# Chunk groups across batches, an accumulator as fifth bank in the last block, and residuals formed by identity products

## The chip, the core and the metric

The kernel runs on one core of a Trainium2 chip. The metric is device microseconds (us) of one execution; the median of three runs is given, and one further execution was profiled. The engines are PE (matmuls; PEld is its weight loads), DVE, ACT, POOL (elementwise work) and SP, which issues nearly all DMAs. Each engine works through its own list of instructions in order.

## The reference, cut to what matters

```
attn: out[b,s,h,:] = sum_k softmax(weight)[h,k] * x[b, s-6+k, h,:]     # B,S,D = 2,4096,192; 8 heads, 7 taps
layer 1: h = x @ w_in;  g = max(0.01*h, h);  x = g @ w_out              # 8192 tokens, 192 -> 2048 -> 192
layer 2: h = x @ w_in2
         P = a0 + a1*h + a2*h^2 + a3*h^3
         Q = 1 + |b0|*|h| + |b1|*h^2
         out = (P / (Q + 1e-6)) @ w_out2
```

All is float32; the weights arrive as 64-bit floats and are converted by the kernel.

## The kernel before, in words

The 8192 tokens are 16 blocks of 512. Hidden units are 16 tiles of 128 (index j). For each block i, layer and tile, `gemm1` (5 matmuls of 128x512) forms the hidden tile h in one of four PSUM banks (pool `bank`), the elementwise engines turn h into a high part gH and a remainder gL (pool `pair`), and `gemm2_hi` (3 matmuls, of gH) and `gemm2_lo` (2, of gL) add them into two accumulators: `acc[0]` in layer 1 (`acc[1]` for block 1), `acc[1]` in layer 2. So a tile costs PE ten matmuls. `middle(i)` (`mid_swap`, `x_hi` on ACT, `mid_add`, `x_lo` on DVE) splits layer 1's result into the operands of layer 2, and `finish(i)` (`fin_*`) transposes and stores layer 2's.

Elementwise work of a layer 2 tile: ACT forms two affine or absolute values of h (`l2_vp`), DVE the denominator's core D (`l2_D`), ACT `l2_abs`, then `l2_rs` and `l2_R` (R = 1/(D+QC)), DVE `l2_p2`, `l2_p3` (numerator without a0, written over h in the bank) and `l2_hi` (gH). The remainder is gL = (h + a0 - (D+QC)*gH) * R: `l2_Q` adds QC to D (ACT or POOL), `l2_w` multiplies by gH (POOL), `l2_r` subtracts (DVE), `l2_lo` multiplies by R (POOL). In the last block (i = 15) the tiles in `GPDEN` form D with `l2_up`, `l2_t` (ACT) and `l2_ut` (POOL) in place of `l2_D` and `l2_abs`; tiles in `ENDW` and `ENDV` may have `l2_w` and `l2_lo` on DVE.

The convolution is a product with a band matrix. Blocks 0 and 1 (`DIRECT`) make it in place; for the rest, chunks of 122 tokens are taken in groups of up to five (`group`): load, `conv_g` (two halves; on PE each is four float32 matmuls, which the trace shows as eight), `evac_g`, and a store to DRAM, from where each block fetches its columns.

The weights come as 28 pieces (14 for each layer): a load, two DVE steps `cv_clip` and `cv_bits` of two instructions each, and splits into high and low parts. Before the first data arrive, `s_warm` runs matmuls on constants.

Order: every step is put into a planner with the engines that it may run on and a rank, made of due times (`LEAD`, `GAP`, `STEP`, `CV1` to `CV3`) and a table of offsets (`OFF`). The planner writes each engine's list once, while the program is built. Layer 2 of a block runs beside layer 1 of the blocks behind it, so the last block's layer 2 has no layer 1 beside it.

## Time and profile before

| | |
|---|---|
| median of 3 runs (lowest, highest) | 1244.76 us (1244.41, 1244.92) |
| profiled execution, whole | 1244.22 us |
| its span in the trace | 1242.4 us |
| mean granted clock of PE, as a share of full speed | 0.996 |
| busy share: PE, DVE, ACT, POOL | 98%, 90%, 92%, 85% |

The span reaches from the first to the last recorded instruction; 1.8 us of the execution lie around it. A matmul's recorded time overlaps the next one's, so 98% for PE does not say that it never waits.

### The profile page before, as it was taken

How to read it: one execution, taken by the hardware profiler on the slowest of the kernel's cores; microseconds unless marked ns; L12 is line 12 of the kernel's file. 1: busy time of each engine (PE TensorE's matmuls, PEld its weight loads, DVE VectorE, ACT ScalarE, POOL GpSimd, SP SyncE). 2: the span in 40 equal slices, each digit the busy share in tenths (PEclk: the TensorE clock that was granted, in tenths of full speed). 3: DMA queues.
4: the chain of work that ended last, by engine and by line, in shares of the span. 5: the costliest groups of instructions: out<-in, count | busy, mean ns of one | idle time of the engine just before them, and what ended most of it. 6: DMA issues, size and time to landing. Idle time of an engine off the chain costs nothing.

```text
span 1242.4 us, 17891 instructions
## 1 busy us (share of the span) xinstructions
PE 1217.3 (98%) x5437; PEld 997.6 (80%) x5437; DVE 1112.0 (90%) x1671; ACT 1138.5 (92%) x1996; POOL 1059.2 (85%) x1000
## 2 busy tenths in 40 slices
PE   8999999999999999999999999999999999999976
PEld 7787788888888888888888888888888888888744
DVE  7999989898998989898988999898998989889898
ACT  6889999899999999999999999999999999999996
POOL 2787988989889898898888989899898888988886
PEclk9999999999999999999999999999999999999998
DMA  7752002020110201111010111010210002000000
GB/s 210 200 164 71 1 3 52 2 42 1 38 18 1 56 1 44 18 30 33 7 45 12 29 33 29 20 23 5 50 26 1 13 1 41 1 1 14 1 13 13
DMA packets 137414, 42.34 MB, mean 34 GB/s; under 512 B 113571, under 2 KB 134758, under 8 KB 137318
## 3 DMA queue, kind: packets, MB, share of 16 engines
q1 hardware_dynamic: 135702, 41.00, 14.3%
q8 instruction: 42, 0.69, 0.2%
q14 instruction: 54, 0.44, 0.1%
q10 hardware_dynamic: 1616, 0.21, 0.1%
HBM read 27.28 MB, written 11.80 MB: 31 GB/s over the span
## 4 chain that ended last, share of the span: by engine, by line
PE 81%; ACT 7%; DVE 7%; issue 2%; DMA 1%; POOL 1%; SPq 0%; POOLq 0%; DVEq 0%; ACTq 0%
PE bank L253 41%; PE acc L253 39%; ACT work L244 4%; DVE work L250 2%; ACT raw L244 1%; DMA raw<-in_moe_w_in_dram 1%; DVE bank L250 1%; DVE pair L247 1%; ACT bank L244 1%; DVE bank L396 1%; DVE bank L397 1%; DVE pair L250 1%; DVE work L247 0%; DVE raw L250 0%; POOL pair L247 0%
## 5 line engine op out<-in xcount | busy, mean ns | idle before, releaser
L253 PE MATMUL acc<-pair,wo 128*128 128x512 f32 x2560 | 657.4, 391 | 6.2 <-POOL pair L247 2.7
L253 PEld LDWEIGHTS acc<-pair,wo 128*128 128x128 f32 x2560 | 478.5, 188 | 110.6 <-POOL pair L247 6.9
L244 ACT ACTIVATE work<-work 128x512 f32<-128x512 f32 x532 | 331.4, 630 | 17.6 <-DVE work L250 11.0
L247 POOL TENSOR_TENSOR work<-work,pair 128x512 f32<-128x512 f32 x184 | 239.5, 1302 | 43.6 <-DVE pair L250 34.6
L253 PE MATMUL bank<-xh,wiH 128*128 128x512 f32 x512 | 203.5, 397 | 9.2 <-DVE raw L250 4.2
L253 PE MATMUL bank<-xh,wiL 128*128 128x512 f32 x512 | 200.2, 391 | 0.0
L253 PE MATMUL bank<-xl,wiH 128*128 128x512 f32 x512 | 200.0, 391 | 0.0
L253 PE MATMUL bank<-xl,wiR 128*128 128x512 f32 x512 | 200.0, 391 | 0.0
L253 PE MATMUL bank<-xh,wiR 128*128 128x512 f32 x512 | 199.9, 390 | 0.0
L250 DVE SCALAR_TENSOR_TENSOR work<-work,b_sb,bank 128x512 f32<-128x512 f32 x182 | 135.1, 742 | 46.5 <-ACT work L244 45.3
L247 POOL TENSOR_TENSOR pair<-work,work 128x512 fp32r<-128x512 f32 x122 | 158.0, 1297 | 20.4 <-DVE work L250 14.8
L250 DVE SCALAR_TENSOR_TENSOR work<-bank,a_sb,work 128x512 f32<-128x512 f32 x184 | 136.9, 744 | 9.6 <-POOL work L247 7.6
L244 ACT ACTIVATE work<-bank,a_sb 128x512 f32<-128x512 f32 x176 | 135.3, 769 | 6.1 <-PE bank L253 6.0
L250 DVE SCALAR_TENSOR_TENSOR pair<-bank,a_sb,work 128x512 fp32r<-128x512 f32 x168 | 125.2, 745 | 13.1 <-ACT work L244 7.8
L250 DVE SCALAR_TENSOR_TENSOR bank<-work,a_sb,bank 128x512 f32<-128x512 f32 x176 | 132.1, 752 | 4.1
L244 ACT ACTIVATE raw<-raw 128x512 f32<-128x512 f32 x202 | 126.8, 630 | 6.2 <-DVE raw L250 3.6
L253 PEld LDWEIGHTS bank<-xh,wiH 128*128 128x128 f32 x512 | 96.4, 188 | 38.1 <-DVE raw L250 6.6
L247 POOL TENSOR_TENSOR pair<-work,pair 128x512 fp32r<-128x512 f32 x92 | 120.3, 1308 | 7.0 <-PE acc L253 1.8
L244 ACT ACTIVATE work<-bank,b_sb 128x512 f32<-128x512 f32 x182 | 124.0, 681 | 0.0
L247 DVE TENSOR_TENSOR work<-work,bank 128x512 f32<-128x512 f32 x176 | 119.3, 678 | 1.3 <-ACT raw L244 1.3
L253 PEld LDWEIGHTS bank<-xl,wiH 128*128 128x128 f32 x512 | 96.5, 189 | 20.7 <-DVE xl L247 0.3
L253 PEld LDWEIGHTS bank<-xl,wiR 128*128 128x128 f32 x512 | 96.4, 188 | 20.6 <-DVE xl L247 0.3
(104 smaller groups left out, 1954.5 us busy)
## 6 DMA issues: line engine op xcount, KB each, us to landing
work<-y_dram SPq DMA_DIRECT2D x108, 64.0 KB
raw<-in_moe_w_out_dram SPq DMA_DIRECT2D x16, 384.0 KB
xt<-in_x_dram SPq DMA_DIRECT2D x59, 96.0 KB
y_dram<-xc SPq DMA_DIRECT2D x58, 84.0 KB
raw<-in_moe_w_in_dram SPq DMA_DIRECT2D x8, 512.0 KB
out_dram<-work SPq DMA_DIRECT2D x63, 64.0 KB
raw<-in_moe_w_in_dram SPq DMA_DIRECT2D x8, 256.0 KB
work<-work SPq DMA_DIRECT2D x16, 128.0 KB
```

The lines of the kernel that those rows point to most:

```text
L244: nc.scalar.activation(out=out_, in_=in_, func=func, **k)
L247: (eng or nc.vector).tensor_tensor(out=out_, in0=in0, in1=in1, op=op)
L250: nc.vector.scalar_tensor_tensor(out=out_, in0=in0, scalar=s, in1=in1, op0=op0, op1=op1)
L253: nc.tensor.matmul(out=out_, lhsT=w, rhs=r, start=start, stop=stop)
L396: nc.vector.tensor_scalar(out=a, in0=a, scalar1=F64_TINY, scalar2=F64_HUGE, op0=ALU.max, op1=ALU.min)
L397: nc.vector.tensor_scalar(out=ai, in0=ai, scalar1=3, scalar2=0x3FFFFFF8, op0=ALU.logical_shift_left, op1=ALU.bitwise_and)
```

## The change

- Chunks are listed over both batches first and then cut into groups of five, so a group may hold the end of batch 0 and the start of batch 1. There are 12 groups; before there were 13, five of them with four chunks.
- The warm-up is 13 float32 matmuls on constants in place of 8 and 19 others; the copy that fed the others (`s_seed`, DVE) goes.
- `s_abs` (ACT, waits for the load of b) stands behind more of ACT's first work.
- When layer 1's last block is through, `acc[0][0]` joins the pool `bank` as a fifth bank.
- In the last block, for the tiles in `QPE`, two matmuls with negated identities subtract QC*gH from h in the bank, and `l2_Q` falls away. For those in `WPE`, one float32 matmul with a negated identity subtracts D*gH there, and `l2_end` (DVE) forms gL in place of `l2_r` and `l2_lo`.
- `GPDEN` has eight tiles for four, `ENDW` and `ENDV` eight for one and two; the numbers that make the ranks are others throughout.

```diff
-LEAD = 66.057
-GAP = 6.373
-PREP = 56.276
+LEAD = 75.81
+GAP = 3.101
+PREP = 36.864
...
-CV1, CV2, CV3 = -20.785, 58.237, 26.634
+CV1, CV2, CV3 = -15.913, 176.158, 29.877
...
-GPDEN = (2, 5, 8, 11)
-ENDW = (15,)
+GPDEN = (0, 1, 2, 3, 5, 9, 12, 14)
+ENDW = (1, 2, 4, 5, 7, 9, 12, 14)
...
-ENDV = (14, 15)
+ENDV = (0, 1, 5, 6, 7, 8, 11, 15)
+QPE = (5, 6, 9, 10, 11)
+WPE = (0, 1, 3, 6, 7, 9, 10, 11, 13)
...
+    pl.pool("own", acc[0][0:1])
...
+    groups = [chunks[c:c + NTC] for c in range(0, len(chunks), NTC)]
...
     def s_warm(eng):
         for n in range(WARM):
             mm(acc[0][1][:, 0:WIDE], ident, qc[:, 0:WIDE], True, True)
-        t = xh[1][0][0]
-        for cols, count, step in SHAPES:
-            for n in range(count):
-                k = n * step % 4
-                mm(acc[0][1][:, 0:cols], t[:, k * P:(k + 1) * P], t[:, 0:cols], True, True)
...
+    def l2_sub(eng, i, j, part):
+        h = b("h", 1, i, j)
+        if part:
+            nc.tensor.matmul(out=h, lhsT=neg, rhs=b("D", 1, i, j), start=False, stop=True, skip_group_check=True)
+        else:
+            for t in negQ:
+                nc.tensor.matmul(out=h, lhsT=t, rhs=b("gH", 1, i, j), start=False, stop=True, skip_group_check=True)
+
+    def l2_end(eng, i, j):
+        stt(b("gL", 1, i, j), b("h", 1, i, j), a_sb[:, 0:1], b("R", 1, i, j), ALU.add, ALU.mult)
...
-            on(DVE(t_dve(n, 1)), s, 9.6, l2_r, i, j, r=[h, dk], w=[dk])
-            on(POOL(t_pool(n)) + end, s, 10.6, l2_lo, i, j, r=[dk, rk], w=[gl], take=("pair", gl))
+            if subw:
+                on(PE(2 * (0.0025 + n / 1200.0)), s, 9.6, l2_sub, i, j, 1, r=[dk, "neg"], w=[h])
+                on(DVE(t_dve(n, 1)), s, 10.6, l2_end, i, j, r=[h, rk], w=[gl], take=("pair", gl))
+            else:
+                on(DVE(t_dve(n, 1)), s, 9.6, l2_r, i, j, r=[h, dk], w=[dk])
+                on(POOL(t_pool(n)) + end, s, 10.6, l2_lo, i, j, r=[dk, rk], w=[gl], take=("pair", gl))
```

Three places of the order show what moves.

The first is SP's list of loads behind the third piece of layer 1's `w_in`; `moe2` names layer 2's weights, `moe` layer 1's, `y_dram` and `xt` belong to the convolution. Before:

```order
L373 DMA raw2_128<-in_moe_w_in_dram 128x1024
L377 DMA raw0_126<-in_moe2_w_in_dram 64x1024 x2
L511 DMA work4_107<-y_dram 32x16x32 x4
L511 DMA work7_110<-y_dram 32x16x32 x4
L373 DMA raw1_127<-in_moe2_w_in_dram 128x1024
L379 DMA raw2_128<-in_moe_w_out_dram 128x2x384
L379 DMA raw0_126<-in_moe_w_out_dram 128x2x384
```

And of the change, behind the same load of `w_in` and ten stores of the first group:

```order
L389 DMA raw0_129<-in_moe_w_out_dram 128x2x384
L484 DMA xt0_79<-in_x_dram 128x192 x5
L521 DMA work7_113<-y_dram 32x16x32 x4
L521 DMA work9_115<-y_dram 32x16x32 x4
L389 DMA raw1_130<-in_moe_w_out_dram 128x2x384
L387 DMA raw2_131<-in_moe2_w_in_dram 64x1024 x2
L383 DMA raw0_129<-in_moe2_w_in_dram 128x1024
```

The pieces of layer 2 have moved behind two of layer 1's output weights, and DVE converts the pieces in the order of their loads.

The second is DVE around the last `x_lo` (the rows `xl101` and `xl111`), where block 15 enters layer 2; the row with `acc01` is `mid_add`, a row `pair<-bank` is an `l2_hi`, a row `work<-bank` or `raw<-bank` an `l2_r`, and rows with `b_sb` are `l2_D`. Before:

```order
L250 SCALAR_TENSOR_TENSOR pair0_116<-bank2_101,a_sb_65,raw0_126 128x512
L247 TENSOR_TENSOR work11_114<-work11_114,acc01_96 128x512
L247 TENSOR_TENSOR work3_106<-work3_106,bank0_99 128x512
L247 TENSOR_TENSOR xl101_92<-acc00_95,xh101_84 128x512
L247 TENSOR_TENSOR xl111_94<-work11_114,xh111_86 128x512
L250 SCALAR_TENSOR_TENSOR work7_110<-bank2_101,a_sb_65,work7_110 128x512
L250 SCALAR_TENSOR_TENSOR bank0_99<-work3_106,a_sb_65,bank0_99 128x512
L250 SCALAR_TENSOR_TENSOR pair1_117<-bank0_99,a_sb_65,raw1_127 128x512
L250 SCALAR_TENSOR_TENSOR work2_105<-work2_105,b_sb_66,bank3_102 128x512
```

Of the change:

```order
L251 TENSOR_TENSOR work2_108<-work2_108,acc01_99 128x512
L254 SCALAR_TENSOR_TENSOR pair8_127<-bank2_104,a_sb_68,raw2_131 128x512
L254 SCALAR_TENSOR_TENSOR raw0_129<-bank3_105,a_sb_68,raw0_129 128x512
L251 TENSOR_TENSOR xl101_95<-acc00_98,xh101_87 128x512
L251 TENSOR_TENSOR xl111_97<-work2_108,xh111_89 128x512
L254 SCALAR_TENSOR_TENSOR raw1_130<-bank2_104,a_sb_68,raw1_130 128x512
L251 TENSOR_TENSOR work12_118<-work12_118,bank0_102 128x512
```

Two steps of block 14 stand ahead of the last `x_lo` in place of one, and one of its steps stands behind it in place of four.

The third is PE in the middle of the last block; rows with `wi` are a `gemm1`, rows `acc<-pair` are `gemm2`, rows with `neg` or `negQ` are the new subtractions. Before, the ten matmuls of `gemm2` for two tiles, with the `gemm1` of another between:

```order
L253 MATMUL acc11_98<-pair5_121,wo1_75 128x512
L253 MATMUL acc10_97<-pair5_121,wo1_75 128x512
L253 MATMUL acc10_97<-pair8_124,wo1_75 128x512 x2
L253 MATMUL acc11_98<-pair8_124,wo1_75 128x512
L253 MATMUL bank2_101<-xh101_84,wiH1_69 128x512
L253 MATMUL bank2_101<-xh101_84,wiL1_71 128x512
L253 MATMUL bank2_101<-xl101_92,wiH1_69 128x512
L253 MATMUL bank2_101<-xh111_86,wiR1_73 128x512
L253 MATMUL bank2_101<-xl111_94,wiR1_73 128x512
```

Of the change, ahead of the `gemm1` of tile 12 (it is the row behind the last one here):

```order
L364 MATMUL bank3_105<-work9_115,neg_65 128x512
L257 MATMUL acc10_100<-pair3_122,wo1_78 128x512 x2
L257 MATMUL acc11_101<-pair3_122,wo1_78 128x512
L367 MATMUL bank2_104<-pair2_121,negQ0_66 128x512
L367 MATMUL bank2_104<-pair2_121,negQ1_67 128x512
L257 MATMUL acc11_101<-pair8_127,wo1_78 128x512
L257 MATMUL acc10_100<-pair8_127,wo1_78 128x512
L257 MATMUL acc10_100<-pair9_128,wo1_78 128x512 x2
L257 MATMUL acc11_101<-pair9_128,wo1_78 128x512
L364 MATMUL bank2_104<-work8_114,neg_65 128x512
L367 MATMUL bank0_102<-pair1_120,negQ0_66 128x512
L367 MATMUL bank0_102<-pair1_120,negQ1_67 128x512
```

PE's list holds the subtractions of tiles 7, 9 and 10 between the hidden products of tiles 11 and 12.

## Rows read from the trace of the kernel before

**Rows 1.** The page's busy times: engine, us, share of the span, instructions.
```profile
PE 1217.3 (98%) x5437; PEld 997.6 (80%) x5437; DVE 1112.0 (90%) x1671; ACT 1138.5 (92%) x1996; POOL 1059.2 (85%) x1000
```

**Rows 2.** Busy us (x instructions) by stretch: PE, PEld, DVE, ACT, POOL; PE's clock, DMA.
```profile
40.00:160.00 120.00, 117.53 (x514) 93.78 (x513) 111.70 (x179) 110.20 (x204) 98.80 (x105) 1.00 0.35 97
200.00:1100.00 900.00, 899.83 (x4048) 745.86 (x4047) 807.82 (x1196) 840.04 (x1463) 796.37 (x739) 1.00 0.11 21
1175.03:1236.90 61.87, 49.11 (x176) 32.87 (x174) 57.43 (x87) 55.07 (x94) 52.35 (x45) 0.94 0.04 7
...
1191.10:1194.30 3.20, 2.98 (x7) 2.37 (x8) 3.20 (x6) 2.27 (x5) 3.07 (x3) 0.50 0.00 0
...
1176.10:1206.50 30.40, 24.15 (x86) 16.17 (x86) 28.68 (x46) 28.63 (x49) 25.86 (x23) 0.94 0.08 14
```

**Rows 3.** The chain that ended last: start us, us, what.
```profile
53.65 0.66 DVE pair L247
...
105.23 1.28 ACT L244
...
142.25 1.45 PE bank L253 x5
...
236.77 2.27 PE bank L253 x10
```

**Rows 4.** PE's waits from 36 to 160 us: us in total, times, longest.
```profile
PE bank L253 <- ACT xc L244: 1.2, 2, 0.9
```

**Rows 5.** PE's timeline at two chunk groups: start, us, operation, count.
```profile
104.07 1.01 PE L253 MATMUL bank<-xt,band 128*122 128x120 f32 x8
104.84 0.94 PE L253 MATMUL acc<-pair,wo 128*128 128x512 f32 x3
...
182.73 1.85 PE L253 MATMUL bank<-xt,band 128*122 128x96 f32 x16
184.36 0.93 PE L253 MATMUL acc<-pair,wo 128*128 128x512 f32 x3
```

**Rows 6.** The timeline of the first 15 us, PE and one step of ACT.
```profile
2.50 5.70 PE L253 MATMUL acc<-qc,ident 128*128 128x256 f32 x16 [2.50 <-POOL ident masks.py:199]
7.84 3.01 PE L253 MATMUL acc<-xh 128*128 128x192 f32 x19
12.22 2.09 PE L253 MATMUL bank<-xt,band 109*103 109x120 f32 x16 [1.36 <-DMA b_sb<-in_moe_b_dram]
13.63 0.20 ACT L244 ACTIVATE b_sb<-b_sb 128x2 f32<-128x2 f32 x1 [2.74 <-DMA b_sb<-in_moe_b_dram]
14.15 0.60 PE L253 MATMUL acc<-qc,ident 128*128 128x256 f32 x2
14.59 0.98 PE L253 MATMUL bank<-xt,band 109*103 109x120 f32 x8
```

**Rows 7.** PE's timeline in the last block; in brackets the idle time before.
```profile
1184.95 0.96 PE L253 MATMUL acc<-pair,wo 128*128 128x512 f32 x3 [2.18 <-DVE work L699]
1191.32 0.79 PE L253 MATMUL bank<-xh,wiH 128*128 128x512 f32 x1 [1.60 <-DVE raw L250]
1211.64 0.80 PE L253 MATMUL bank<-xh,wiH 128*128 128x512 f32 x1 [1.74 <-DVE raw L250]
1224.92 0.39 PE L253 MATMUL bank<-xl,wiR 128*128 128x512 f32 x1
```

**Rows 8.** DVE's timeline: last `x_lo`, tile 6's `l2_r`, tile 15's `l2_lo`.
```profile
1175.43 0.68 DVE L247 TENSOR_TENSOR xl<-work,xh 128x512 fp32r<-128x512 f32 x1
1205.76 0.75 DVE L250 SCALAR_TENSOR_TENSOR work<-bank,a_sb,work 128x512 f32<-128x512 f32 x1
1235.29 0.79 DVE L247 TENSOR_TENSOR pair<-raw,work 128x512 fp32r<-128x512 f32 x1
```

**Rows 9.** The last `fin_swap`, and SP's last stores.
```profile
1236.68 0.59 ACT L244 ACTIVATE work<-acc 64x512 f32<-64x512 f32 x1 [4.00 <-PE acc L253]
1237.66 1.65 SPq L720 DMA_DIRECT2D out_dram<-work  x3
```

84 lines of the change are left out of this document (45 added, 39 removed).

## The prediction

> **What bounds the kernel now.** I read the page's busy times first: PE 98%, ACT 92%, DVE 90%, POOL 85% [rows 1]. PE leads, but the share is an average, so the next view is busy time by stretch. From 200 to 1100 us PE is busy for 899.8 of 900 us and starts 4048 matmuls, one in 0.222 us [rows 2]. There only fewer matmuls can save anything. From 40 to 160 us it starts 514; at 0.222 us the 120 us would hold 540, so 26 matmuls, 5.7 us, are lost [rows 2]. In the last block, 1175.0 to 1236.9 us, PE starts 176 [rows 2]: 168 at 0.227 us (ten in 2.27 us [rows 3]) are 38.1 us, 8 of the constant kind at 0.22 us (two in 0.44 us: starts at 14.15 and 14.59 [rows 6]) 1.8 us, so 39.9 us of work and 22.0 us without. DVE is busy for 57.4 of these 61.9 us, ACT for 55.1.
>
> The third view is the chain that ended last. From about 54 to 142 us its pieces are mostly DVE's, from 142 us PE's [rows 3]: the first stage is held by DVE, which converts weights beside layer 1's remainders. So there are three places for a gain: the start, PE's list in the middle, and the last block.
>
> **The change part by part.** Durations are those of the profiled execution, 1244.22 us whole, of which 1242.4 are the span; it lies 0.5 us below the median of 1244.76, and the sum is carried over to that.
>
> *One chunk group fewer.* The number of chunks stays at 60. Eight matmuls over five chunks take 0.77 us until the next one starts, sixteen over four chunks 1.63 us, 0.82 for eight [rows 5]: a product with fewer chunks costs PE the same. Where PE is dense, a group less is therefore a whole 1.63 us, and with the two changes of operand about 1.7. **-1.7 us** (1.6 to 1.9). A chunk of batch 1 in the same group needs one small clearing on DVE more, in slack of the dense stretch.
>
> *The start: the warm-up.* PE's 16 constant matmuls begin at 2.50 us, 19 others at 7.84, and PE is idle for 1.36 us until the convolution at 12.22, which waits for a load [rows 6]. The new warm-up is 26 of the constant kind: ten more at 0.22 us from 7.84 end near 10.1, so the idle time grows to about 2.1 us. What the clock does then is open. In the last block the granted clock fell to half (0.50 from 1191.1 to 1194.3 [rows 2]) after PE had been idle for 1.60 us, and matmuls ran long again after 1.74 us; after 2.18 us it held, and that idle time stood behind dense work [rows 7]. Two of three such gaps were followed by half speed, so I take that: the second half of the convolution's 2 us runs at half, which puts its end about 1.0 us back. The Trainium skill, "TensorE: Matmul & The Clock Gate", section "What's actually happening", says that "the default state is throttled, and activity releases the throttle"; by it the longer pause speaks against the change, as two of the rows do and one does not. If the clock holds, the term is a gain of 0.4 us: ACT no longer sits until 13.63 us in `s_abs` [rows 6], ahead of the first evacuation. **+1.0 us** (-0.4 to +1.3). The removed copy of DVE (`s_seed`) lies under ACT's table load.
>
> *The start: conversions.* In the order, 58 DVE steps stand up to `l1_lo[0,11]` before and 53 now, 67 and 62 up to `l1_lo[1,11]`, 107 and 89 up to `l1_lo[2,3]`; what goes back are layer 2's conversions, and layer 2 itself begins some 30 matmuls later on PE. That takes four to five instructions and more off the engine that holds the chain from 54 to 142 us. At most all 5.7 us come back. Not all will: 1.2 us of PE's waits are for the evacuation of a chunk group on ACT [rows 4], behind ACT's table load of 1.28 us at 105.2 [rows 3], and that load comes with layer 2's first `l2_rs` in either order; with the restarts I leave 1.7. **-4.0 us** (-5.7 to -1.0, the low end if another wait follows at once). The conversions put off lie behind 142 us beside a PE-bound stretch in which DVE has some 10% to spare: 807.8 of 900 us [rows 2].
>
> *The middle.* Between `gemm1` and `gemm2_hi` of a tile stand as many matmuls of other tiles as before or a few more (medians 9 to 10 us of PE's work before and 12 to 13 now in layer 1, 17 to 18 and 18 to 20 in layer 2), so I expect no new waits: 0.
>
> *The last block, engine work.* Behind the last `x_lo` DVE has 77 instructions up to tile 15's `l2_lo`, before 85: four `l2_D` and one `l2_w` are gone, three steps of block 14 have moved ahead. ACT loses eight of its nine `l2_Q`. PE gains nine float32 subtractions, twice the width of the constant kind, 0.88 us each, and ten f32r ones: 7.9 + 2.3 = 10.2 us, 50.1 of some 61. So DVE and ACT are relieved and PE is loaded.
>
> *The last block, in three pieces.* (a) Ahead of the last `x_lo` now stand `l2_hi` and `l2_r` of block 14 in place of one `l2_p2`, and on ACT two steps of tile 15 ahead of `mid_swap`: +1.1 us. (b) From the end of the last `x_lo` (1176.1) to that of `l2_r[15,6]` (1206.5) DVE did 44 instructions in 30.4 us, 0.69 each [rows 2, 8]. Now `l2_end[15,6]`, which frees the bank for tile 11's `gemm1`, is the 42nd: 29.0 us, and about 0.7 more because only one step is left to cover the wait for tile 0: 29.7. From there PE's list up to tile 15's `gemm1` holds 60 matmuls of the usual kind (13.6 us), four wide subtractions (3.5) and six others (1.4): 18.5 us with no gap that a bank could fill. Behind it the last tile's steps take as long as now, from 1225.3 (1224.92 + 0.39 [rows 7]) to 1236.1 [rows 8], 10.8 us. Together 59.0 us against 60.0: -1.0. (c) `fin_add` now comes ahead of `fin_main` and so waits for `fin_swap`, 0.59 us long [rows 9], of which I count 0.35, since PE's last matmul ends inside it; and SP's last store stands behind that of the transposed rest, 0.55 us each (1.65 for three [rows 9]): +0.9. Sum **+1.0 us**; DVE without any wait would give -9 in (b), PE with its old idle time +10.
>
> Sum: -1.7 + 1.0 - 4.0 + 1.0 = -3.7 us. 1244.22 - 3.7 = 1240.5 on the profiled scale, 1241.1 as a median.
>
> **The rivals.**
> - *The fifth bank frees the last block.* PE's longest waits there are of `gemm1` for DVE's last reader of a bank [rows 7]. If PE's list doesn't bind, DVE does its 77 instructions at 0.66 us (57.43 / 87 [rows 2]), 50.8 us, with the 3.9 us of waits that it has now (60.0 - 85 x 0.66): 54.7, so (b) is -5.3, the sum -8.0 and the median 1236.8. For it: the bank is there when it is needed. Against it: the subtractions stand in front of those very `gemm1`. The Trainium skill, "Trainium Kernel Development and Optimization", section "Best Practices", says that consistent bubbles can mean that PSUM ran out; the trace agrees for the waits before 1191.3 and 1211.6 us. By that rule the sum would be the one just given.
> - *The start's wait only moves.* Loads and ACT's conversions may hold layer 1 where DVE did. Then 1.0 us comes back there in place of 4.0: sum -0.7, median 1244.1, no change to be told. For it: ACT also waits for loads in that stage; against it: DVE's pieces make up the chain.
> - *PE binds the last block (slower).* Each subtraction waits for POOL's `l2_w`, and behind it in PE's list wait the `gemm2` and `gemm1` of other tiles. My sum leaves PE 10.8 us of idle time (60.9 - 50.1). At 14.5 us the gain is gone, and if all 22.0 stay the kernel is 7.5 us slower. Halfway, at 18, it is +3.5: median 1248.3. Against it: dense work keeps the clock up, and both drops of now cost PE time.
>
> **How the numbers follow.** 0.2% (2.5 us) is about what a measurement of this kernel can tell from no change. Forecast 0.45, of which 0.38 faster by more than that and 0.07 within it; the fifth bank 0.20 (faster); the wait that moves 0.20 (0.18 within, 0.02 faster); PE 0.15 (0.13 slower, 0.02 within). So faster 0.60, same 0.27, slower 0.13. The forecast's own range is 1238 to 1244. The range for 8 in 10 takes in the second and third case and leaves out most of the last and the low side of the second: 1236 to 1246.
>
> **What would show it.** Twelve groups, each 1.63 us of PE: 192 matmuls on `xt,band` of 122 rows. PE's clock at half somewhere between 13 and 17 us, or not. In 40 to 160 us more than 530 matmuls, and no long run of DVE pieces in the chain there. In the last block PE dense from about 30 us behind the last `x_lo` for some 18 us, DVE with waits in that stretch, and the whole from there to `l2_lo` near 59 us. I am wrong if PE's idle time in the last block is above 15 us, if waits appear between 200 and 1100 us, or if 40 to 160 us holds no more matmuls than now.

## The result, and the profile after

The changed kernel is slower: 1252.15 us (median of 6, 1250.22 to 1252.98) against 1244.84 us (median of 6), ratio 1.0056 [1.0043, 1.0069]. That is 7.3 us more, and 11 us above the prediction of 1241.1. The profiled execution took 1251.42 us, 7.20 more than that of before; 1249.6 us are its span, and its mean granted clock is 0.996 as before.

The page's busy times of the changed kernel, in the order of [rows 1] (us, share, instructions):

```profile
PE 1224.2 (98%) x5440; PEld 999.4 (80%) x5440; DVE 1109.6 (89%) x1667; ACT 1139.2 (91%) x1977; POOL 1060.6 (85%) x1009
```

Every share is the same or a point lower than before: the page says nothing of where 7 us went. Busy time by stretch does, with the columns of [rows 2]:

```profile
40.00:160.00 120.00, 117.77 (x521) 95.62 (x520) 108.34 (x174) 106.87 (x196) 94.48 (x99) 1.00 0.37 101
200.00:1100.00 900.00, 897.68 (x4017) 740.13 (x4016) 809.69 (x1203) 843.50 (x1455) 802.06 (x749) 1.00 0.10 21
1177.97:1242.90 64.93, 55.60 (x203) 37.34 (x201) 53.82 (x80) 49.66 (x84) 48.42 (x43) 0.97 0.04 7
```

From 200 to 1100 us PE starts 4017 matmuls where it started 4048 [rows 2], although a group less should leave room for more of the usual ones. A stretch in which I had expected nothing is the largest loss.

To say how much, I measured PE by the starts of its matmuls: the **loss** of a stretch is the sum, over neighbouring matmuls, of the time from start to start less the usual one (0.227 us for 512 columns, 0.097 for one of a chunk group, 0.44 for a wide subtraction). With two milestones, the start of layer 1's last `gemm2_lo` and that of layer 2's, the span falls into stages. All runs of this study, in us ("last block" is from one milestone to the other, "end" from there to the end of the span):

| kernel | first gemm1 | loss 20–160 | loss 160–1100 | last block | end | median | ratio to before |
|---|---|---|---|---|---|---|---|
| before | 17.8 | 6.8 | 3.7 | 64.5 | 6.3 | 1244.84 | |
| after | 18.7 | 5.4 | 8.9 | 67.9 | 7.3 | 1252.15 | 1.0056 [1.0043, 1.0069] |
| x1_groups | 21.0 | 8.2 | 6.3 | 64.6 | 6.2 | 1246.20 | 1.0013 [1.0003, 1.0023] |
| x2_old_ranks | 17.3 | 7.1 | 6.2 | 66.2 | 6.2 | 1248.09 | 1.0026 [1.0017, 1.0035] |
| x3_old_last | 19.5 | 5.4 | 8.8 | 68.2 | 7.4 | 1252.37 | 1.0060 [1.0046, 1.0074] |
| x4_old_warm | 18.5 | 5.1 | 8.9 | 67.4 | 7.3 | 1251.27 | 1.0051 [1.0037, 1.0065] |
| x5_lo_later | 20.1 | 7.8 | 4.6 | 63.4 | 6.2 | 1244.49 | 0.9997 [0.9986, 1.0008] |
| x6_tail | 18.4 | 5.4 | 8.8 | 64.2 | 7.3 | 1248.97 | 1.0035 [1.0023, 1.0047] |
| x7_bank_alone | 17.7 | 7.4 | 4.6 | 62.0 | 6.2 | 1242.03 | 0.9978 [0.9968, 0.9988] |
| x8_old_off | 17.8 | 8.4 | 16.1 | 66.8 | 6.2 | 1260.02 | 1.0121 [1.0103, 1.0140] |
| x9_pairs | 18.0 | 5.6 | 8.6 | 68.0 | 7.3 | 1252.36 | 1.0063 [1.0049, 1.0078] |
| x10_no_products | 18.3 | 5.2 | 8.8 | 69.5 | 7.6 | 1252.34 | 1.0064 [1.0052, 1.0076] |
| x11_warm | 17.9 | 7.7 | 4.6 | 61.8 | 6.2 | 1241.43 | 0.9978 [0.9969, 0.9987] |
| x12_mix | 17.8 | 8.3 | 4.6 | 63.2 | 6.2 | 1243.63 | 0.9998 [0.9987, 1.0008] |
| x13_six_tiles | 19.6 | 6.4 | 8.8 | 67.9 | 7.3 | 1253.06 | 1.0069 [1.0057, 1.0081] |
| x14_tail_wide | 17.6 | 6.6 | 4.6 | 63.5 | 6.2 | 1243.67 | 0.9991 [0.9981, 1.0000] |
| x15_tail_close | 17.8 | 8.6 | 4.7 | 64.1 | 6.2 | 1242.85 | 0.9992 [0.9984, 1.0001] |
| x16_lead | 19.7 | 13.9 | 15.8 | 67.0 | 7.4 | 1270.25 | 1.0211 [1.0187, 1.0234] |
| x17_two_later | 18.1 | 5.2 | 7.9 | 67.5 | 7.3 | 1249.82 | 1.0047 [1.0034, 1.0059] |
| x18_six_later | 19.4 | 5.5 | 10.3 | 66.7 | 7.3 | 1253.85 | 1.0076 [1.0062, 1.0090] |

The stages are from one profiled execution each, the medians from several. The loss from 160 to 1100 us repeats to 0.1 us where the list is the same (8.8 to 8.9 in the change, x3, x4, x6 and x10; 4.6 to 4.7 in x5, x7, x11, x12, x14 and x15). That from 20 to 160 varies by 2 us between like lists (6.6 to 8.6 in those with the old numbers), and the last block by about 1 us (64.6 and 63.4 in x1 and x5). Read by stage, before to after: +0.8 to the first `gemm1`; then +1.9 to layer 1's last `gemm2_lo`, which is -1.6 for the group, -1.4 in the first 160 us, +5.2 from 160 to 1100, and -0.3 elsewhere; +3.4 in the last block; +1.0 at the end. Sum +7.1, and the spans differ by 7.2.

PE's waits from 160 to 1100 us (total us, times, longest), first of before and then of the changed kernel:

```profile
PE bank L253 <- DVE pair L247: 0.2, 1, 0.2
```
```profile
PE bank L257 <- DVE pair L251: 2.3, 6, 1.0
```

All six are a `gemm1` whose bank was last read by an `l1_lo` on DVE. The longest of them in the timeline (start, us, engine, operation; in brackets the idle time before):

```profile
723.89 1.30 POOL L251 TENSOR_TENSOR pair<-work,work 128x512 fp32r<-128x512 f32 x1
723.99 1.75 DVE L251 TENSOR_TENSOR xl<-work,xh 128x512 fp32r<-128x512 f32 x1
...
726.31 0.68 DVE L251 TENSOR_TENSOR pair<-bank,pair 128x512 fp32r<-128x512 f32 x1
...
727.05 0.50 PE L257 MATMUL bank<-xh,wiH 128*128 128x512 f32 x1 [1.00 <-DVE pair L251]
```

The second `x_lo` of block 9 takes 1.75 us, not 0.68 as in [rows 8]; the `l1_lo`, two steps behind it in DVE's list, frees the bank, and PE waits 1.00 us (1.16 by the starts of its matmuls).

In the last block, the rows of PE and DVE that answer to [rows 7] and [rows 8] (the second of DVE is `l2_end` of tile 6):

```profile
1211.16 0.50 PE L257 MATMUL bank<-xh,wiH 128*128 128x512 f32 x1 [1.55 <-DVE pair L254]
1230.06 0.39 PE L257 MATMUL bank<-xl,wiR 128*128 128x512 f32 x1
1233.19 1.36 PE L257 MATMUL acc<-pair,wo 128*128 128x512 f32 x3 [2.28 <-DVE pair L254]
```
```profile
1179.02 0.80 DVE L251 TENSOR_TENSOR xl<-work,xh 128x512 fp32r<-128x512 f32 x1
1210.37 0.73 DVE L254 SCALAR_TENSOR_TENSOR pair<-bank,a_sb,work 128x512 fp32r<-128x512 f32 x1
1241.24 0.95 DVE L251 TENSOR_TENSOR pair<-raw,work 128x512 fp32r<-128x512 f32 x1
```

The three parts of (b) are 31.3 us (1179.82 to the end of `l2_end[15,6]` at 1211.10), 19.35 (to 1230.45) and 11.7 (to 1242.19): 62.4 against the forecast's 59.0. The end, as in [rows 9]:

```profile
1242.78 0.59 ACT L248 ACTIVATE work<-acc 64x512 f32<-64x512 f32 x1 [6.16 <-PE acc L257]
...
1244.74 1.60 SPq L730 DMA_DIRECT2D out_dram<-raw  x3
```

### The profile page after: what moved, and what is told of

Read it like the earlier page. It is cut to its first block, busy times and chain, and to the rows that moved or that the text cites. A ratio compares the mean times of both kernels' runs of the same rounds, so it can differ in the third digit from the quotient of the medians.

```text
span 1249.6 us, 17818 instructions
## 1 busy us (share of the span) xinstructions
PE 1224.2 (98%) x5440; PEld 999.4 (80%) x5440; DVE 1109.6 (89%) x1667; ACT 1139.2 (91%) x1977; POOL 1060.6 (85%) x1009
## 4 chain that ended last, share of the span: by engine, by line
PE 83%; DVE 6%; ACT 6%; issue 2%; POOL 1%; DMA 1%; SPq 1%; POOLq 0%; DVEq 0%; ACTq 0%
PE bank L257 42%; PE acc L257 40%; ACT work L248 3%; DVE pair L254 2%; ACT raw L248 2%; DVE work L254 1%; DVE bank L254 1%; DVE raw L254 1%; DVE pair L251 1%; DVE raw L251 0%; DVE work L251 0%; ACT bank L248 0%; POOL raw L251 0%; DMA xt<-in_x_dram 0%; DMA b_sb<-in_moe_b_dram 0%
## 5 line engine op out<-in xcount | busy, mean ns | idle before, releaser
L257 PE MATMUL acc<-pair,wo 128*128 128x512 f32 x2560 | 639.1, 391 | 6.5 <-DVE pair L254 3.8
L248 ACT ACTIVATE work<-work 128x512 f32<-128x512 f32 x508 | 316.6, 629 | 22.9 <-DVE work L254 12.8
L251 POOL TENSOR_TENSOR work<-work,pair 128x512 f32<-128x512 f32 x179 | 232.8, 1302 | 42.5 <-DVE pair L254 38.6
L251 POOL TENSOR_TENSOR pair<-work,work 128x512 fp32r<-128x512 f32 x117 | 152.5, 1305 | 12.0 <-DVE work L254 9.1
L254 DVE SCALAR_TENSOR_TENSOR pair<-bank,a_sb,work 128x512 fp32r<-128x512 f32 x186 | 138.6, 746 | 21.7 <-ACT work L248 9.3
L254 DVE SCALAR_TENSOR_TENSOR work<-work,b_sb,bank 128x512 f32<-128x512 f32 x173 | 128.3, 742 | 31.1 <-ACT work L248 30.0
L254 DVE SCALAR_TENSOR_TENSOR work<-bank,a_sb,work 128x512 f32<-128x512 f32 x171 | 127.2, 745 | 7.3 <-POOL work L251 6.0
L251 POOL TENSOR_TENSOR raw<-raw,pair 128x512 f32<-128x512 f32 x77 | 100.7, 1308 | 25.3 <-DVE pair L254 19.5
L248 ACT ACTIVATE raw<-raw 128x512 f32<-128x512 f32 x182 | 113.5, 627 | 7.4 <-DVE raw L254 5.3
L248 ACT ACTIVATE work<-bank,b_sb 128x512 f32<-128x512 f32 x173 | 117.8, 681 | 0.0
```

The source lines that it names most:

```text
L248: nc.scalar.activation(out=out_, in_=in_, func=func, **k)
L251: (eng or nc.vector).tensor_tensor(out=out_, in0=in0, in1=in1, op=op)
L254: nc.vector.scalar_tensor_tensor(out=out_, in0=in0, scalar=s, in1=in1, op0=op0, op1=op1)
L257: nc.tensor.matmul(out=out_, lhsT=w, rhs=r, start=start, stop=stop)
```

## The experiments

"The old numbers" are before's `LEAD`, `GAP`, `PREP`, `STEP`, `PULL`, `WINDOW`, `REST`, `OFF`, `TAIL` and `CV1` to `CV3`; "the new lists" are the new `GPDEN`, `ENDW`, `ENDV`, `QPE`, `WPE`.

**x1: the chunk groups alone**, in the kernel before.

```diff
+    groups = [chunks[c:c + NTC] for c in range(0, len(chunks), NTC)]
+    spans = [(g[0][0] * S + g[0][1] + g[0][2], g[-1][0] * S + g[-1][1] + CG) for g in groups]
```


> The kernel before with only the chunk groups of the change (12 of five chunks). Theory: one group fewer is worth 1.7 us of PE and nothing else moves, so 1243.1 us beside 1244.8 for the kernel before. Rival: groups that cross the batches, or their new places in the order, bring the waits that the changed kernel shows between 160 and 1100 us; then PE loses some 9 us there in place of 3.7, and the time is 1247 us or more.

1246.20 us: 1.6 more, not 1.7 less. The loss from 160 to 1100 us is 6.3, before 3.7; PE's waits there have two new entries:

```profile
PE bank L253 <- DVE work L250: 1.9, 2, 1.1
```

At one of them the timeline shows

```profile
566.60 2.52 POOL L247 TENSOR_TENSOR xl<-work,xh 128x512 fp32r<-128x512 f32 x2
568.07 1.61 DVE L247 TENSOR_TENSOR xl<-work,xh 128x512 fp32r<-128x512 f32 x1
569.60 0.74 DVE L250 SCALAR_TENSOR_TENSOR work<-bank,a_sb,work 128x512 f32<-128x512 f32 x1
570.39 0.50 PE L253 MATMUL bank<-xh,wiH 128*128 128x512 f32 x1 [1.12 <-DVE work L250]
```

An `x_lo` with both operands in SBUF, begun while POOL was in an instruction, took 1.61 us; the `l2_r` behind it frees the bank for PE. Such meetings are not new by themselves. The kernel before has them too, at block 9 as an example,

```profile
722.57 1.53 DVE L247 TENSOR_TENSOR xl<-work,xh 128x512 fp32r<-128x512 f32 x1
```

and at blocks 4 and 10 (1.47 and 1.54 us), and PE waits behind none of them; x1 keeps these three and waits only at blocks 7 and 13. A meeting costs PE time where the reader of the next bank stands right behind it. In this execution the first `gemm1` also came 3.2 us late, since the convolution ran at half clock (section on the hardware).

**x2: the changed kernel with the old numbers.**

```diff
-LEAD = 75.81
+LEAD = 66.057
...
-TAIL = 3.475
+TAIL = 5.502
-CV1, CV2, CV3 = -15.913, 176.158, 29.877
+CV1, CV2, CV3 = -20.785, 58.237, 26.634
```


> The changed kernel with all the numbers of the ranks (LEAD, GAP, PREP, STEP, PULL, WINDOW, REST, OFF, TAIL, CV1 to CV3) of the kernel before; groups, warm-up, fifth bank and subtractions stay. Theory: the 5.2 us that PE lost anew between 160 and 1100 us come from the order that the new numbers make on DVE (l1_lo behind x_lo), so they go: 1252.1 - 5.2 = 1247 us, or 1248.3 if the stage from 20 to 160 us loses its 1.4 us of gain too; the last block is open by 2 us. Rival: a part of the change in the code (groups, bank) makes the waits; then PE still loses some 9 us from 160 to 1100 us and the time stays at 1251 to 1253 us.

1248.09 us, 4.1 less than the change. The loss from 160 to 1100 us is 6.2, that of x1: of the middle's 5.2 us, 2.5 come with the groups and 2.7 with the numbers. This split goes by one path: the new numbers with the old groups were not run, and x2 has x1's two waits for an `l2_r`, of which the changed kernel has none. The end is back at 6.2, the first 160 us lose 7.1 again, and the last block takes 66.2.

**x3: the changed kernel with before's lists and without the fifth bank.**

```diff
-GPDEN = (0, 1, 2, 3, 5, 9, 12, 14)
-ENDW = (1, 2, 4, 5, 7, 9, 12, 14)
+GPDEN = (2, 5, 8, 11)
+ENDW = (15,)
...
-QPE = (5, 6, 9, 10, 11)
-WPE = (0, 1, 3, 6, 7, 9, 10, 11, 13)
+QPE = ()
+WPE = ()
```


> The changed kernel with the last block's settings of before (no fifth bank, no subtractions on PE, GPDEN, ENDW and ENDV of before); all other numbers stay, and the order up to the last block is the same instruction for instruction. Theory: the bank, the subtractions and the two lists together cost 3.3 us there, since the subtractions fill PE while DVE still waits; without them 1248.8 us. Rival: the new offsets and TAIL make the last block slow by themselves; then 1252 us or more. A third: the parts do help and the numbers hurt; then above 1254 us.

The last block takes 68.2 us without the bank and the products, 67.9 with them, 64.5 with the old numbers and lists. So with the new numbers the block is 3.7 us longer before any of the new work is in it.

**x4: the changed kernel with before's warm-up.**

```diff
-WARM = 13
+WARM = 8
+SHAPES = ((192, 6, 1), (384, 3, 1), (512, 3, 1), (256, 3, 1), (192, 4, 0))
```


> The changed kernel with the warm-up matmuls of before (16 constant ones and 19 on a copied tile, with the copy on DVE); the order is otherwise the same instruction for instruction. Theory of the prediction: the shorter warm-up puts the first convolution and all behind it back by 1.0 us; then 1251.1 us and the convolution starts at 12.2 us. Rival, from the trace of after: the clock was granted in full there, and the convolution started 0.8 us later because its load landed later; the warm-up has no part in it, the time stays at 1252.1 us, and the convolution starts when the load lands, whenever that is.

1251.27 against 1252.15: the intervals overlap, so the warm-up's own worth can't be told here; they allow anything from 3 us of loss to 1.5 of gain for the change's.

**x5: as x1, with two neighbours of DVE's list exchanged**, `x_lo[1,7,1]` and `x_lo[1,13,1]` with the step behind each.

```diff
+    for i in (7, 13):
+        a = next(p for p, (n, e) in enumerate(order) if pl.ops[n].get("step") == ("x_lo", 1, i, 1))
+        z = next(p for p in range(a + 1, len(order)) if order[p][1] == "DVE")
+        order.insert(z, order.pop(a))
```


> The kernel before with the chunk groups of the change, and on DVE two neighbours exchanged at two places: l2_r of block 6's tile 5 goes ahead of block 7's second x_lo, and l2_r of block 12's tile 13 ahead of block 13's; all other lists are those of the kernel with the groups alone. Theory: PE's two new waits there (1.1 and 0.8 us) are for those l2_r, which stood behind an x_lo that took 1.61 and 1.52 us in place of 0.68 because a POOL instruction was running; with the exchange both are gone, PE loses some 4.0 us from 160 to 1100 us in place of 6.3, and the time is 1246.2 - 2.2 = 1244.0 us on the scale where the kernel before has 1244.6. Rival: the data of the new groups come late (block 8 starts batch 1), and gemm1 waits for the next thing at the same places; then 1246 us.

1244.49 us, 1.7 less than x1, and the loss falls from 6.3 to 4.6. At the place shown above:

```profile
566.59 0.74 DVE L250 SCALAR_TENSOR_TENSOR work<-bank,a_sb,work 128x512 f32<-128x512 f32 x1
567.25 0.95 DVE L247 TENSOR_TENSOR xl<-work,xh 128x512 fp32r<-128x512 f32 x1
567.60 1.75 POOL L247 TENSOR_TENSOR pair<-work,work 128x512 fp32r<-128x512 f32 x1
567.65 0.39 PE L253 MATMUL bank<-xh,wiH 128*128 128x512 f32 x1
569.41 0.73 PE L253 MATMUL acc<-pair,wo 128*128 128x512 f32 x2 [0.47 <-POOL pair L247]
```

The `gemm1` waits no more, but POOL's instruction, which now begins inside `x_lo`, takes 1.75 us where it takes 1.30 by itself, and PE waits 0.47 us for that one. The exchange does two things at once: `l2_r` no longer stands behind `x_lo`, and `x_lo` meets less of POOL's instruction. That the added length did it is arithmetic (0.93 us of the wait of 1.12), not a run of its own. The group is worth nothing measurable even so: 0.9997, though the interval reaches from a gain of 1.7 us to a loss of 1.0.

**x6: the changed kernel with before's `TAIL`**, the distance of the due times of layer 2's tiles once layer 1 is through.

```diff
-TAIL = 3.475
+TAIL = 5.502
```


> The changed kernel with TAIL, the spacing of the last block's ranks, of before (5.502 for 3.475); the order is the same up to the last block. With the old ranks the last block (from the last gemm2_lo of layer 1 to that of layer 2) took 64.6 us with the old settings and 66.3 with the new, with the new ranks 68.2 and 68.0. Theory: TAIL is what makes it slow, since closer ranks let steps of later tiles pass those of the tile that holds the bank; then it takes some 66.3 us and the time is 1250.4 us. Rival: the offsets of the steps do it; then 68 us and 1252 us.

The last block takes 64.2 us for 67.9, the kernel 3.2 us less than the change (2.6 by the ratios). One number is worth most of that stage's loss. Some 1.3 us of the 3.7 need not be its own: the clock fell late in the changed kernel's block and not in x6's, as told below under the last block.

**x7: as x5, with the fifth bank alone.**

```diff
+    pl.pool("own", acc[0][0:1])
...
+        if i + 3 == NB:
+            on(POOL(0.01), t1[-1], 9.0, lambda eng: None, w=[("acc", 0, 0), "own"], take=("own", "own"),
+               retire=("own", "bank", lambda t: [t]))
```


> The kernel of x5_lo_later with the fifth bank joined for the last block and nothing else of the last block's change (no subtractions, the lists of before). Up to the last block the order is the same. Theory (the first rival of the prediction on its own): with a fifth bank the waits of gemm1 for DVE's last reader shrink, the last block takes 61 to 63 us in place of 64.6, and the time is 1241 to 1242.5 us. Rival: DVE, busy for 57 of 62 us, sets the pace whatever the banks; then 64 to 65 us and the time of x5_lo_later.

1242.03 us, 0.9978 of before: the first kernel that is faster. The last block takes 62.0 us, 2.5 less than before and 1.4 less than x5.

**x8: the changed kernel with before's `OFF`.**

```diff
-OFF = {'xfin_add': 7.81, 'xfin_main': -19.87, 'l2_rs': -69.42,
...
+OFF = {'xfin_add': 27.93, 'xfin_main': -41.19, 'l2_rs': -6.51,
```


> The changed kernel with the table OFF of before; LEAD, GAP, PREP, STEP, PULL, WINDOW, REST, TAIL and CV1 to CV3 stay as changed. Theory: OFF is what puts layer 1's l1_s, l1_hi and l1_lo behind layer 2's steps on ACT and DVE, so that a bank of layer 1 is held for 4.8 us at the median in place of 3.9; with the old table the hold is 3.9 us again, PE loses 4 to 6 us from 160 to 1100 us in place of 8.9, and the end after PE's last matmul takes 6.2 us in place of 7.2. Rival: GAP and the other numbers do it, since they set how far layer 2 runs beside layer 1; then the hold stays at 4.8 us.

The end is 6.2 again, as expected, and DVE's tiles of layer 1 hold their banks for 3.9 us again (median; 4.8 in the changed kernel). But the loss from 160 to 1100 us is 16.1 and the time 1260.02: the shorter hold does not shorten the waits.

**x9: the changed kernel with an eleventh buffer in `pair`**, dealt anew over the same order.

```diff
+    pairs = [const.tile([P, FB], F32R, name=f"pair{n}") for n in range(N_PAIR + EXTRA)]
...
+    for n, e in order:
+        o = pl.ops[n]
+        for p, (k, _) in enumerate(o["slot"]):
+            if k in left:
+                holds[k] = idle.pop(0)
```


> The changed kernel with eleven pair buffers in place of ten (room for it from the unread half of the constant tile). The order is planned with ten and stays the same on every engine; only the buffers are dealt out again over eleven. Theory: with the new numbers gemm2 stands further behind gemm1, a pair is held longer (7405 us of 9000 from 200 to 1100 us in place of 6941), so l1_hi and l1_lo wait for a pair that PE has not yet read, layer 1 holds its bank for 4.8 us in place of 3.9, and gemm1 waits for the bank. With eleven, PE's loss from 160 to 1100 us falls from 8.9 to 5 to 6 us and the time from 1252.1 to 1249 us. Rival: l1_s, l1_hi and l1_lo are late because layer 2's steps stand ahead of them on ACT and DVE; then the hold and the waits stay, 1252 us.

(The counts 7405 and 6941 in this expectation are too low; by the traces pairs are held for some 7900 us in the changed kernel and 7400 in the kernel before.) POOL's waits for a pair from 200 to 1100 us, of the changed kernel and of x9:

```profile
POOL pair L251 <- PE acc L257: 14.8, 24, 1.4
```
```profile
POOL pair L253 <- PE acc L259: 4.7, 7, 1.3
```

Of 14.8 us of waits 10.1 are gone, and PE loses 8.6 as against 8.9, its six waits for `l1_lo` still 2.2 us. Buffers are not the cause.

**x10: as x6, without the products** (`l2_sub`).

```diff
-QPE = (5, 6, 9, 10, 11)
-WPE = (0, 1, 3, 6, 7, 9, 10, 11, 13)
+QPE = ()
+WPE = ()
```


> The kernel of x6_tail (the changed kernel with TAIL of before) without the subtractions on PE: QPE and WPE empty, l2_Q, l2_r and l2_lo again for all tiles; fifth bank, GPDEN, ENDW and ENDV as changed. The order up to the last block is the same. Theory: the subtractions add 10.2 us to PE's list and take only 5 l2_Q from ACT and some l2_lo from POOL or DVE, so without them the last block takes no longer, 62 to 64 us in place of 64.2, and the time is 1247 to 1249 us. Rival: they relieve the engines that set the pace; then 66 us or more and 1251 us.

The last block takes 69.5 us for 64.2. In windows over the block (x6 first, then x10) POOL's busy time, the fifth of the engines, goes from 49.4 to 58.5:

```profile
1174.10:1238.30 64.20, 57.58 (x218) 38.84 (x217) 57.57 (x86) 53.29 (x89) 49.43 (x44) 1.00 0.04 7
```
```profile
1173.80:1243.30 69.50, 54.92 (x190) 40.30 (x189) 60.44 (x88) 56.02 (x94) 58.52 (x51) 0.83 0.03 6
```

With eight tiles in `GPDEN`, which give POOL `l2_ut`, the products take `l2_lo` off it; that POOL sets the pace is argued from these sums. A rival is left: PE's granted clock is 1.00 over the block in x6 and 0.83 in x10 (the third number from the end of each row), and no run separates the two.

**x11 and x12: x7 with a longer warm-up; x7 with four products.**

```diff
-WARM = 8
+WARM = 10
```


> The kernel of x7_bank_alone with two more constant float32 matmuls in the warm-up (WARM 10 for 8): PE's idle time ahead of the first convolution, 0.7 to 2.2 us in the profiles so far, shrinks by some 0.9 us. Theory: the longer idle times let the clock fall to half (granted 0.50 after 2.15 us in two profiles and after 1.59 in one, 1.00 after 1.88 in another), which costs 2 to 3 us in those executions; with the shorter idle time no execution has it, the slowest ones go, and the median falls by 0.2 to 0.8 us below 1242.0. Rival: the clock's fall is rare enough not to move the median, and the warm-up now ends behind the load; then 1242.0 to 1242.5 us.

```diff
-GPDEN = (2, 5, 8, 11)
+GPDEN = (1, 2, 4, 5, 7, 8, 10, 11)
...
+WPE = (1, 4, 7, 10)
```


> The kernel of x7_bank_alone with four more tiles whose D is formed on ACT and POOL (GPDEN 1, 2, 4, 5, 7, 8, 10, 11) and, for tiles 1, 4, 7 and 10, the float32 subtraction of D*gH on PE with l2_end in place of l2_r and l2_lo. In x7 DVE is busy for 57.1 of the last 59.3 us, POOL for 52.5, PE for 49.5. Four l2_D fewer take 2.6 us from DVE, POOL's four products and four l2_lo cancel, PE gains 3.4 us. Theory: DVE sets the pace, so the last block takes 60 us in place of 62.0 and the time is 1240.5 us. Rival: the subtractions stand in PE's list ahead of gemm1 and gemm2 of other tiles and hold the bank longer; then 62 to 64 us, 1242 to 1244 us.

x11: 1241.43 us, 0.9978, not to be told from x7. x12: 1243.63 us, and the last block 63.2 for 62.0; beside the old order the products and the longer `GPDEN` cost about 1 us of the block and 2 of the kernel (0.9998 for 0.9978) instead of helping.

**x13: as x9, with 14 steps of six tiles of layer 1** (those that wait at block entries) put one to four places earlier on ACT and DVE.

```diff
+    for step, i, j, places in (("l1_s", 7, 3, 1), ("l1_s", 8, 5, 1), ("l1_s", 10, 3, 3), ("l1_s", 14, 3, 1),
...
+        ahead = [q for q in range(p) if order[q][1] == order[p][1]][-places]
+        order.insert(ahead, order.pop(p))
```


> The kernel of x9_pairs (the changed kernel, eleven pair buffers) with the order changed by hand for the six tiles of layer 1 whose bank PE waits for between 400 and 1040 us: l1_s and l1_hi one to three places earlier on ACT, l1_lo one to four places earlier on DVE, 14 moves in all; the lists of PE, POOL and SP are the same. More pairs alone did nothing. Theory: layer 1's steps are late because layer 2's steps stand ahead of them on ACT and DVE; with the moves those banks come free 1 to 2.5 us earlier, at least four of the six waits go, PE loses 6 us from 160 to 1100 us in place of 8.6, and the time is 1249.8 us in place of 1252.4. Rival: both engines are late by themselves there (ACT 94% busy, DVE 90%), so the layer 2 steps that are moved back bring waits of the same length for layer 2's banks; then 8 to 9 us are lost as before, 1252 us.

Loss 8.8, with x9 8.6: some waits went to other `gemm1`, some stayed, and the sum did not fall, as the rival said.

**x14 and x15: x11 with `TAIL` 6.5, and with the change's 3.475.**

```diff
-TAIL = 5.502
+TAIL = 3.475
```


> The kernel of x11_warm (the order numbers and lists of before, twelve chunk groups, fifth bank, longer warm-up; 1241.4 us) with TAIL 6.5 in place of 5.502. The order up to the last block is the same. Theory: with wider ranks a tile's steps are finished before the next tile's begin and the banks come free earlier, which was worth 3.8 us from 3.475 to 5.502; a further point is worth less, 0 to 1.5 us: 1240 to 1241.4 us. Rival: too wide a spacing leaves the engines waiting for one tile's chain; then 1242 us or more.

> The kernel of x11_warm with TAIL 3.475, the value of the change, in place of 5.502. Theory: TAIL alone costs the last block some 3.8 us, as it did with the offsets of the change: 65.5 us in place of 61.8, 1245 us. Rival: it costs that only together with the change's offsets; then 1241.5 us.

The last block is 61.8 us at 5.502, 63.5 at 6.5 and 64.1 at 3.475, in one execution each. The same 3.475 costs 2.3 us here, beside the old numbers and lists, and 3.7 in x6. By the ratios either value costs 1.6 to 1.7 us of the kernel, and the intervals just touch that of x11.

**x16: the changed kernel with before's `LEAD`.**

```diff
-LEAD = 75.81
+LEAD = 66.057
```


> The changed kernel with LEAD, the rank at which layer 2 begins, of before (66.057 for 75.81); all other numbers stay. In the order 17 tiles of layer 2 then stand ahead of layer 1's block 3 on PE, in place of 13 now and 16 in the kernel before; 222 stand ahead of block 15 in all three. Theory: in the change layer 2 begins three tiles later and has to be caught up between 160 and 1100 us, where it loads ACT and DVE more than layer 1's tiles do, and PE pays with the 5.2 us of waits; with the old LEAD PE loses 4 to 6 us there in place of 8.9, while from 20 to 160 us the gain of 1.4 us is gone: 1249 to 1250.5 us. Rival: the waits come from the order at a block's entry, whatever layer 2's start; then 8 us or more are lost from 160 to 1100 us, 1252 us or more.

Loss 13.9 and 15.8 and 1270.25 us, 18 more than the change: the theory is refuted. Neither `OFF` nor `LEAD` can be put back singly; each is fitted to the others.

**x17 and x18: the changed kernel with late `x_lo`.** In x17 the second `x_lo` of blocks 5 and 9 stands two places later, behind the `l1_lo` that PE waits for; in x18 those of blocks 6, 7, 12 and 13 stand one place later too.

```diff
+    for i, places in ((5, 2), (9, 2)):
+        a = next(p for p, (n, e) in enumerate(order) if pl.ops[n].get("step") == ("x_lo", 1, i, 1))
+        z = [p for p in range(a + 1, len(order)) if order[p][1] == "DVE"][places - 1]
+        order.insert(z, order.pop(a))
```


> The changed kernel with the second x_lo of blocks 5 and 9 (DVE) moved two places later, behind the l1_lo for which gemm1 waits there. In the profile of the changed kernel these two x_lo took 1.75 us each in place of 0.68, since POOL's instruction of 1.30 us began 0.1 us earlier, and gemm1 waited 0.35 and 1.16 us for the l1_lo behind them. Theory: the lengthened x_lo is a part of the middle's 5.2 us also in the changed kernel; then these two waits are gone, PE's loss from 160 to 1100 us falls from 8.9 to about 7.4, PE's waits for l1_lo there from 2.3 us to about 1.0, and the median from 1252.1 to about 1250.6. Rival: layer 1's tiles hold their banks too long whatever stands ahead of l1_lo; then the same or another gemm1 waits as long and the loss stays at 8.5 to 9, the median at 1252.

> As the run with two, and the second x_lo of blocks 6, 7, 12 and 13 moved one place later too; in the profile of the changed kernel these took 1.47, 1.65, 1.63 and 1.47 us, and gemm1 waited 0.42, 0.38, 0.59 and 0.16 to 0.39 us some 6 to 8 us behind them. Theory: as far as the new places lie clear of POOL's instructions, these waits go too: loss 6 to 7, median 1249.5 to 1250.5. An x_lo that meets another POOL instruction there is as long as before and its wait stays, so that the waits which go should be those behind an x_lo that got shorter. Rival: the loss stays at 8.5 to 9, or waits go and come without regard to the length of the x_lo ahead of them.

x17 at block 9, the place shown in the result:

```profile
722.60 1.31 POOL L251 TENSOR_TENSOR pair<-work,work 128x512 fp32r<-128x512 f32 x1
723.19 0.75 DVE L254 SCALAR_TENSOR_TENSOR raw<-raw,b_sb,bank 128x512 f32<-128x512 f32 x1 [0.41 <-ACT raw L248]
723.85 0.69 DVE L251 TENSOR_TENSOR pair<-bank,pair 128x512 fp32r<-128x512 f32 x1
724.46 0.68 DVE L251 TENSOR_TENSOR xl<-work,xh 128x512 fp32r<-128x512 f32 x1
```

`x_lo` begins behind POOL's instruction and takes 0.68 us. The waits of 0.35 and 1.16 us at the two blocks are gone, a new one of 0.50 stands behind the second, and the loss falls by 1.0 where I had expected 1.5. 1249.82 us lies 2.3 below the change, but the intervals of the ratios overlap, so the stage tells it and the time does not. In x18 the move of block 13 went wrong:

```profile
1033.94 1.29 POOL L251 TENSOR_TENSOR pair<-work,pair 128x512 fp32r<-128x512 f32 x1
1034.00 1.78 DVE L251 TENSOR_TENSOR xl<-raw,xh 128x512 fp32r<-128x512 f32 x1
1035.70 0.74 DVE L254 SCALAR_TENSOR_TENSOR work<-bank,a_sb,work 128x512 f32<-128x512 f32 x1
...
1036.59 0.47 PE L257 MATMUL bank<-xh,wiH 128*128 128x512 f32 x1 [1.31 <-DVE work L254]
```

Begun 0.06 us inside POOL's instruction, `x_lo` took 1.78 us for 1.47 and the `gemm1` behind the next `l2_r` waits 1.31 us: loss 10.3. In block 6 `x_lo` got shorter (0.68 us) and the wait behind it stayed (0.45 us). The expectation puts the wait of 0.59 us behind block 12's `x_lo`, and that is wrong: it stands at 883.6 us, behind block 11's, which took 0.68 us in both kernels, and PE waits for nothing behind block 12's 1.63 us. So an `x_lo` ahead of the `l1_lo` makes the waits of blocks 5 and 9: they go when it moves (shown). That its added length does it, and not its place alone, is arithmetic: 1.07 us for a wait of 1.16. The waits of blocks 6 and 11 have another cause.

## Why the prediction was wrong, by its own steps

**The middle, 0, is the step that failed most: +5.2.** I argued from the number of matmuls between `gemm1` and `gemm2_hi`, which measures how long PE can wait for a tile's product; what ended the waits was the last reader, on DVE, of the *bank* that the next `gemm1` needs. By x1 and x2, 2.5 of the 5.2 come with the new groups, at an `x_lo` that meets a POOL instruction (moving it takes 1.7 of them back, x5), and 2.7 with the new numbers. In the changed kernel itself all the waits are for an `l1_lo`, and 1.0 of its loss goes when `x_lo` moves at blocks 5 and 9 (x17). For the rest, 1.7 of the numbers' share, the cause stays open: banks are held 0.9 us longer in the median, but a shorter hold (x8), more buffers (x9), earlier tiles (x13) and a shorter `x_lo` (x18, block 6) did not take the waits away.

**One group fewer, -1.7.** The price was right: from 200 to 1100 us matmuls of chunk groups fall from 160 to 144, 1.6 us by [rows 5]. That it would be "a whole 1.63 us" failed: a group in another place shifts DVE's list against POOL's, and with the new meetings 2.5 are lost again (x1). I had looked for slack for the chunk's own steps, not at what their new place does to their neighbours.

**The start, +1.0, had nearly the right size (+0.8) by the wrong mechanism, which is luck.** The clock held: the granted clock is 1.00 over the convolution of the changed kernel, after 1.88 us of idle time, and the rows are

```profile
2.40 8.71 PE L257 MATMUL acc<-qc,ident 128*128 128x256 f32 x26 [2.40 <-POOL ident masks.py:199]
13.00 1.86 PE L257 MATMUL bank<-xt,band 109*103 109x120 f32 x16 [1.88 <-DMA b_sb<-in_moe_b_dram]
```

The convolution began at 13.00 for 12.22 [rows 6], since its load landed later, and no moved step was found that explains it: over the executions profiled here it began between 11.7 and 13.0 us, with either warm-up. The forecast's idle time was wrong too: the new warm-up ended at 11.11 us (2.40 + 8.71) and not near 10.1, since its matmuls came one in 0.43 us up to 8.1 us and one in 0.22 only behind that. The term -0.4 for a clock that holds was not seen either.

**The conversions, -4.0, were mis-sized: -1.4.** The mechanism is there: every kernel with the new numbers but x13 and the two misfits x8 and x16 loses 5.1 to 5.6 us from 20 to 160, those with the old ones 6.6 to 8.6. The kernel before, with 6.8, is at the low end of these; on the means of the two sets the gain is 2.3 us, still short of 4.0. From 40 to 160 us PE starts 521 matmuls for 514, not the 530 I had asked for. What took the conversions' place, in PE's waits from 36 to 160 us:

```profile
PE bank L257 <- DVE pair L251: 1.2, 2, 0.9
PE acc L257 <- DVE pair L251: 1.0, 1, 1.0
PE bank L257 <- DVE wiR L251: 0.4, 1, 0.4
```

Mostly `l1_lo` on DVE, where [rows 4] had an evacuation on ACT: the engine that held the stage still holds it, with its own work of layer 1. I had left 1.7 us of the 5.7 for such waits, and they kept 4.3 (5.7 - 1.4).

**The last block, +1.0, came to +4.4** with its end. (a) +0.9 for +1.1, and (c) +1.0 for +0.9, were right; x8 shows the second by itself, 6.2 us with before's `OFF`. (b) was -1.0 and measured +2.4, its three parts 1.6, 0.9 and 0.9 us too long. In the first, DVE did not run its 42 instructions at 0.69 us without a wait: rows of DVE right behind the last `x_lo` are

```profile
1181.70 0.69 DVE L251 TENSOR_TENSOR work<-work,bank 128x512 f32<-128x512 f32 x1 [1.23 <-ACT work L248]
...
1184.05 0.72 DVE L709 STREAM_TRANSPOSE work<-acc 128x512 f32<-128x512 f32 x1 [0.87 <-PE acc L257]
```

2.1 us where I had allowed for 0.7. The second part was as dense as foreseen, without one wait of PE's behind the `gemm1` at 1211.16, but its matmuls took 19.35 us where my prices gave 18.5. In the third the clock fell. PE had been idle for 2.28 us (the row at 1233.19), the granted clock was 0.50 from 1233.6 to 1236.9, and DVE, ahead of the last tile's steps, waited for tile 13's subtraction:

```profile
1236.04 1.49 PE L364 MATMUL acc<-work,neg 128*128 128x512 f32 x2
1237.57 0.75 DVE L254 SCALAR_TENSOR_TENSOR pair<-acc,a_sb,raw 128x512 fp32r<-128x512 f32 x1 [1.28 <-PE acc L364]
```

x18 has the same lists in this stretch and the same idle time, 2.29 us. There the clock held at 1.00, the subtraction took

```profile
1237.19 1.02 PE L364 MATMUL acc<-work,neg 128*128 128x512 f32 x2
```

DVE did not wait for it, and the part took 10.5 us; so it did in x13. In x4, x9 and x17, where the clock fell, it took 11.3 to 11.8. So 10.8 was right for a clock that holds, and the fall, which my sum did not have in the last block, is worth 0.8 to 1.3 us. What makes the block slow against the kernel before lies beside the bank and the products: with the new numbers it takes 68.2 without them (x3), and with before's `TAIL` it takes 3.7 us less (x6). I had read the order's rows for single steps and not asked what the new spacing does to the whole block.

**The rivals.** *The fifth bank frees the last block* gave 1236.8; its mechanism was right, as x7 shows beside the old order (62.0 us for 63.4 to 64.6), at a quarter to a half of the price (1.4 to 2.6 us of 5.3), and the change hides it; beside the old numbers the bank with all the new lists takes 66.2 (x2). *The start's wait only moves* was largely true of that term, to the tune of 1.4 us and not 1.0. *PE binds the last block*: PE's idle time there, by the starts of its matmuls, is 15.2 us, above the 14.5 from which the gain is gone, but the subtractions are not most of it. Of 9.1 us of waits in PE's list from 1178 us on, theirs are these two:

```profile
PE bank L367 <- DVE pair L254: 1.1, 1, 1.1
PE bank L364 <- POOL work L251: 0.5, 1, 0.5
```

The block is shorter with them beside the new numbers (x10: 69.5 without, x6: 64.2 with, at unlike clocks) and 1 us longer beside the old (x12). Two of the three marks that I had named for being wrong came true, waits from 200 to 1100 us and idle time above 15 us; the one on 40 to 160 us did not.

**Which version is best.** x7 and x11: the numbers and lists of before, twelve groups with two neighbours exchanged on DVE, and the fifth bank; 0.9978 of before, so 2 to 3 us faster than it and 10 faster than the change.

## What to carry to other kernels

A change that removes work from a dense stretch also shifts two engines' lists against each other; before counting its gain whole, look at which DVE steps with both operands in SBUF will stand beside a POOL instruction, and above all whether the last reader of the next bank stands behind them; without such a reader the meetings cost PE nothing here. When a change brings new features and new tuning numbers together, run each beside the old of the other: here a good feature (the fifth bank) lay under a bad set of numbers, and a single one of these (`TAIL`) was over a third of the loss. Numbers that were found as a set can be worse than either set when they are put back one at a time.
